# Two factor sets through memory, a finish by banks, and another order of the first phase

## The chip, the cores and the metric

The kernel runs on one core of a Trainium2 chip, in one launch. The time is the device time in microseconds (us) of that core. Five engines work in parallel, each through its own instructions in order, and wait for one another by semaphores: TensorE (PE; its weight loads are shown as PEld), VectorE (DVE), ScalarE (ACT), GpSimd (POOL), and SyncE (SP), which here only issues DMAs. A queue of DMAs belongs to the engine that issues them, and a waiting DMA holds up those behind it in the same queue.

## What is computed

Attention with a block mask, for 8 batches x 8 heads, 576 tokens and a head size of 64, then a two-layer network over all 4608 tokens:

```python
scores = scale * np.matmul(q, k.transpose(0, 1, 3, 2))        # scale = 1 / sqrt(64)
scores = np.where(block_i >= block_j, scores, -1000000000.0)  # blocks of 64 tokens
scores = scores - np.max(scores, axis=-1, keepdims=True)
attn = np.exp(scores)
attn = attn / (np.sum(attn, axis=-1, keepdims=True) + 1e-09)
out = np.matmul(attn, v)
# heads side by side: x is [4608, 512]
h = x @ w_in                                                  # w_in [512, 2048]
g = np.maximum(h, 0.0) + alpha * np.minimum(h, 0.0)
return g @ w_out                                              # w_out [2048, 512]
```

The reference makes the weights in 64 bits; they come as pairs of 32-bit words, and the kernel turns them into 32-bit numbers itself.

## The kernel before, in words

**Numbers.** Matrix products run on a rounded 32-bit format. A number that must not lose precision is split into a high part (a rounding copy, ACT, line 422) and a low part (number minus high part, POOL or DVE, line 423), and a product becomes three: high by high, high by low, low by high. A weight tile of 128 x 512 is first converted by `to_f32` (line 380): a DMA into a `raw` tile, then masks and bit operations on DVE (L398, L403, L406), conversions on ACT (L401, L409), a last multiplication on POOL (L417). One step in between, adding the lower word, has two forms, chosen by the conversion's priority (line 410): below `LOW_POOL` ACT converts the word (L411) and POOL adds it (L412); from there on one DVE instruction does both (L414). `RB`, `EB` and `EF` are the numbers of `raw`, `m` (result) and `ef` (intermediate) tiles.

**First phase.** 32 pairs of heads go through attention, one after another: scores on PE (L815), row maximum on DVE (L820), exchange of half rows on POOL (L792), exponential with row sum on ACT (L828), block transposes on DVE (L832), product with v on PE (L874). Four half pairs are done ahead of the loop, with priorities from `E0` and `E1`. `PM`, `PX`, `PT`, `PZ` and `PU` are priorities of the single steps against their pair, `VL` that of the load of v. Beside attention, 6 of the 16 blocks of 128 hidden units (`FA = 6`) are computed directly for chunks of 256 tokens (L518, L528, L530, L541, L544, L557), and their part of the result goes to memory (`part`, L750). Their twelve weight tiles are converted at the start (`first_weights`, line 428). The weights of the other ten blocks are converted meanwhile, tile k behind the pair `int(A0 + A1 * k)` (`weights_ahead`, line 444), and written to memory (`wd`). The priority of such a conversion is 5p + 100 where attention for pair p has 5p: it fills gaps.

**Second phase.** The remaining ten hidden blocks are taken as five pairs i = 0 to 4, and both layers use a scheme of seven products in place of eight (quadrants, and sums of quadrants). Each pair needs two factor sets, w1 and w2: two loads from `wd` (L454), four sums of 256 columns on POOL (`add`, L439), and four splits (512, 512, 512 and 256 columns) with the high parts on ACT and the low parts on DVE; a set is 2 x 7 x 256 numbers per partition. `later_weights` (line 457) makes all ten, for i = 0 to 4, w1 and w2 in turn. For each of nine chunks of 512 tokens, `factors` loads x from memory (L574), forms four differences (DVE, L583) and splits seven X factors. `pair1` (line 601) does seven products of six matmuls (L615), adds them up out of PSUM with the help of small `u` tiles (L624, L628, L635) and applies the activation (L528, L530). `parts_of` (line 657) makes from that the parts `ha` and `hs`: four sums of 128 columns (L439) and two splits. `pair2` (line 676) does the second layer's seven products, gathered over the five pairs in four PSUM banks M0/M1, M2/M3, M4/M5, M6 (L684); first the three that use `ha` (M0, M1, M6), then the four that use `hs` (M2 to M5). `finish` (line 693) then takes one copy (L706), seven sums (DVE, L703) and four sums with `part` (L439), and two stores to `out` (L718). In the last half chunk ("tail") the parts use spare X buffers, and the engines of their steps come from `TSADD`, `TALO` and `TSLO` in place of `SADD`, `ALO` and `SLO`.

**Memory.** When the last attention pair is done (`end_attention`, line 933), its memory becomes the pool `wb`: 4 w1 sets, 2 w2 sets, 4 X factors, 11 tiles `t2` (`WB1`, `WB2`, `XB2`, `TB2`). The direct blocks still have three chunks to go then. When these are done (`end_first`, line 947), their memory becomes `fx`: the remaining w1, w2, X and `t2`, `ha`, `hs`, and all 11 `u` tiles. An instruction that writes into new memory waits until the old users have finished, stores included.

**What sets the order.** Every instruction is entered in a plan with engine, cost, what it reads and writes, and a priority (smaller is earlier). `Plan.schedule` (line 140) plays the program through with those costs and takes for each free engine the ready entry of least priority for which buffers are free; the order in which it does so becomes each engine's order of instructions. On the chip an engine keeps this order also where the costs were off. Buffers of the kinds in `IN_ORDER` (line 78), the `mw` tiles of the loads from `wd` among them, are given out in the order in which the entries were made. `due(d)` (line 564) is a priority against the running count of PE's products in the second phase; `UX`, `UX0`, `UF`, `UP`, `UM`, `UO` and `UW` are such offsets, for X factors (`UX0`: those of the first chunk), `pair1`, parts, the sums of `finish`, its last sums, and weights.

## Time and profile before

| | us |
|---|---|
| median of 3 runs (1056.52 to 1058.59) | 1056.69 |
| the profiled execution | 1056.06 |
| its span, first to last instruction | 1054.3 |
| PE busy | 982.9 |
| DVE busy | 867.0 |
| POOL busy | 772.1 |
| ACT busy | 624.6 |

The profile comes from one execution. All times of the trace count from the span's first instruction. L422 is line 422 of the kernel before. Groups are named output<-input by the kernel's buffers, without their numbers: `w` stands for a factor set (w1 or w2), `t` for a `t2` tile, `bank` for a PSUM bank, `duo` for a pair of banks of attention. Matmuls are pipelined and their ends are modelled. What released a waiting instruction is inferred from semaphores; where several were waited for, the last by the profile is named.

### The profile page before, as it was taken

The numbers are of one execution on the slowest core, as the hardware profiler recorded it, in microseconds if no ns is written. First come the engines' busy times: TensorE is split into PE (matmuls) and PEld (weight loads), VectorE is DVE, ScalarE is ACT, GpSimd is POOL, SyncE is SP. The second block draws the span as 40 slices with busy tenths as digits, with TensorE's granted clock in tenths as the row PEclk, the third lists the DMA queues.
The fourth block names the chain that finished last, engine by engine and source line by source line (L and its number), as shares of the span: only waits on it lengthen the run. The fifth ranks groups of instructions, "written<-read, shape, count | busy, mean of one in ns | idle before, by whom it ended". The sixth has DMA issues, their size and how long they took to land. (4 is left out here: it accounts for less than half of the span.)

```text
span 1054.3 us, 34971 instructions
## 1 busy us (share of the span) xinstructions
PE 982.9 (93%) x13670; PEld 902.9 (86%) x13670; DVE 867.0 (82%) x1925; ACT 624.6 (59%) x2158; POOL 772.1 (73%) x1318
## 2 busy tenths in 40 slices
PE   5478999999999999999989799999999999999997
PEld 3366787889888898888878789999999999999996
DVE  6999889988888878866584997888888888888876
ACT  6878687877777676756554654445353545444442
POOL 5887567656566665646598889888887979797963
PEclk7679899999999999999999999999999999999999
DMA  8555667576566566442433202130303031221111
GB/s 311 157 194 172 220 215 239 168 245 204 181 217 224 184 194 204 154 164 77 131 103 110 72 21 81 42 100 22 101 21 100 25 98 44 78 61 62 61 42 60
DMA packets 85045, 135.96 MB, mean 129 GB/s; under 512 B 12176, under 2 KB 49552, under 8 KB 84880
## 3 DMA queue, kind: packets, MB, share of 16 engines
q1 hardware_dynamic: 84592, 133.59, 39.4%
q8 instruction: 107, 1.75, 0.7%
q14 instruction: 58, 0.48, 0.1%
q10 hardware_dynamic: 288, 0.14, 0.0%
HBM read 100.15 MB, written 33.55 MB: 127 GB/s over the span
## 5 line engine op out<-in xcount | busy, mean ns | idle before, releaser
L828 ACT ACTIVATE p<-duo,c 128x256 f32<-128x256 f32 (+8 forms) x576 | 221.1, 415 | 40.7 <-DVE c L823 32.2
L615 PE MATMUL bank<-X,w 128*128 128x256 f32 x1890 | 237.8, 282 | 3.1 <-DMA t<-wd 1.8
L615 PEld LDWEIGHTS bank<-X,w 128*128 128x128 f32 x1890 | 230.5, 190 | 4.3 <-ACT X L422 2.0
L792 POOL TENSOR_SCALAR c<-c 32x4 f32<-32x4 f32 (+3 forms) x400 | 100.6, 252 | 87.0 <-DVE c L820 59.4
L439 POOL TENSOR_TENSOR t<-t 128x128 f32<-128x128 f32 (+1 forms) x180 | 103.3, 583 | 60.5 <-DVE t L530 48.0
L684 PE MATMUL bank<-w,hs 128*128 128x256 f32 x1020 | 138.3, 284 | 5.5 <-POOL hs L423 5.5
L557 PE MATMUL bank<-wa,gh 128*128 128x512 f32 x432 | 137.9, 400 | 3.8 <-POOL gh L539 1.7
L684 PEld LDWEIGHTS bank<-w,hs 128*128 128x128 f32 x1020 | 128.9, 192 | 8.0 <-POOL hs L423 7.7
L828 ACT ACTIVATION_READ_ACCUMULATOR p<-duo,c 128x1 f32 x576 | 130.7, 228 | 0.0
L518 PE MATMUL bank<-xh,wa 128*128 128x256 f32 x864 | 126.7, 289 | 1.5 <-DVE g L530 1.3
L820 DVE TENSOR_REDUCE c<-duo 128x2 f32<-128x512 f32 (+8 forms) x288 | 121.3, 475 | 6.5 <-PE duo L815 6.2
L439 POOL TENSOR_TENSOR t<-t,t 128x128 f32<-128x128 f32 (+1 forms) x200 | 120.8, 609 | 4.0 <-DVE w L423 1.3
L518 PEld LDWEIGHTS bank<-xh,wa 128*128 128x128 f32 x864 | 114.5, 193 | 10.6 <-issue 3.4
L423 POOL TENSOR_TENSOR hs<-t,hs 128x512 fp32r<-128x512 f32 x85 | 112.1, 1319 | 13.2 <-ACT hs L422 13.0
L544 POOL TENSOR_TENSOR gl<-g,gh 128x256 fp32r<-128x256 f32 x108 | 85.1, 790 | 45.6 <-ACT gh L541 14.6
L422 ACT CAST hs<-t 128x512 fp32r<-128x512 f32 x85 | 52.8, 621 | 104.4 <-POOL t L439 103.4
L684 PE MATMUL bank<-w,ha 128*128 128x256 f32 x765 | 104.9, 283 | 5.8 <-DVE ha L423 5.8
L832 DVE STREAM_TRANSPOSE PTH<-p 128x576 f32<-128x576 f32 (+4 forms) x160 | 99.7, 630 | 11.6 <-ACT p L828 10.4
L815 PE MATMUL duo<-k,q 64*32 64x288 f32 (+4 forms) x2560 | 85.7, 382 | 22.6 <-ACT p L828 18.5
L684 PEld LDWEIGHTS bank<-w,ha 128*128 128x128 f32 x765 | 97.4, 191 | 6.2 <-DVE ha L423 6.2
L528 ACT ACTIVATE u<-bank 128x256 f32<-128x256 f32 x180 | 64.1, 382 | 62.6 <-DVE bank L628 62.3
L557 PEld LDWEIGHTS bank<-wa,gh 128*128 128x128 f32 x432 | 77.2, 188 | 22.7 <-issue 3.3
(69 smaller groups left out, 1913.2 us busy)
## 6 DMA issues: line engine op xcount, KB each, us to landing
v<-in_v SPq DMA_DIRECT2D x32, 576.0 KB, 4.2
k<-in_k SPq DMA_DIRECT2D x32, 288.0 KB, 5.3
t<-xd SPq DMA_DIRECT2D x36, 256.0 KB, 4.1
t<-part SPq DMA_DIRECT2D x36, 256.0 KB, 2.7
out<-t SPq DMA_DIRECT2D x36, 256.0 KB, 2.1
va<-in_v SPq DMA_DIRECT2D x32, 256.0 KB, 3.3
raw<-in_w_in SPq DMA_DIRECT2D x16, 512.0 KB, 5.3
raw<-in_w_out SPq DMA_DIRECT2D x16, 512.0 KB, 4.3
```

The source lines that it names most:

```text
L423: op(on, c_pool(n) + 60 if on == "POOL" else Beside(c_dve(n)), lambda: (nc.gpsimd if on == "POOL" else nc.vector).tensor_tensor(out=lo(), ...
L439: op(e, c_pool(n) if e == "POOL" else Beside(c_dve(n)), lambda: (nc.gpsimd if e == "POOL" else nc.vector).tensor_tensor(out=to[1](), in0=a ...
L518: nc.tensor.matmul(hp()[:, :n], ww()[:, 0, cc * P:(cc + 1) * P], x()[:, cc, :n], start=(i == 0 and cc == 0), stop=(i == 2 and cc == NCC - 1))
L544: op("POOL", c_pool(CHA) + 60, lambda: nc.gpsimd.tensor_tensor(out=gl(), in0=g(), in1=gh().bitcast(F32), op=ALU.subtract), r=[g, gh], w=[g ...
L557: nc.tensor.matmul(acc(), a()[:, ts], ww(), start=(first and i == 0), stop=(last and i == 2))
L615: nc.tensor.matmul(bank()[:, :CHA], W()[:, i, 256 * at + P * c:256 * at + P * c + P], B()[:, j, CHA * c:CHA * c + CHA], start=(n == 0), st ...
L684: nc.tensor.matmul(accs[n // 2]()[:, CHA * (n % 2):CHA * (n % 2) + CHA], b()[:, u, P * x:P * x + P], W()[:, v, 256 * W2AT[w]:256 * W2AT[w] ...
L792: nc.gpsimd.tensor_scalar(out=o, in0=i, scalar1=scale, scalar2=None, op0=ALU.mult)
L815: nc.tensor.matmul(sb()[32 * i:32 * i + 32, h, off[T]:off[T] + w], q()[hs, qs], blocks(k()[hs], T + 1, 32 * (i % 2)), start=True, stop=True)
L820: op("DVE", c_dve(2 * w), lambda t=t, w=w, o=o: nc.vector.tensor_reduce(out=c()[:, 0, 2 * t:2 * t + 2], in_=sb()[:, :, o:o + w], axis=AX.X ...
L828: op("ACT", 237 + w / 1.2, lambda x=2 * t + h, T=T, h=h, w=w, o=o: nc.scalar.activation(out=pb()[:, 2 * o + h * w:2 * o + h * w + w], in_= ...
L832: op("DVE", 85 + 2.08 * w, lambda to=to, a=a, w=w, o=o: nc.vector.transpose(out=to()[:, a:a + 2 * w], in_=pb()[:, 2 * o:2 * o + 2 * w]), r ...
```

## The change

**Stored factor sets.** `AGAIN` names two sets, w2 of pair 4 and w2 of pair 3. `later_weights`, now called after `end_first` has been entered, makes these two first, then the other eight in the old order. Each of the two is written to memory (`wf`) in two DMAs when it is complete, its buffer becomes free, and two DMAs fetch it into another w2 buffer once the old phase's memory is free (the key "fa"). The pool `wb` has 3 w1 sets, 2 w2 sets, 6 X factors, 12 `t2` and 2 `u` tiles; `fx` has the rest, the totals staying as they were. `XB` and `UX0` move the first chunk's X factors, `XWHEN` the loads of x for later chunks by one pair, `UX` and `UF` shift two priorities.

**Finish bank by bank.** In the last half chunk's last pair, `pair2` enters four groups of products, one for each bank, in place of two. In the last half chunk `finish` gives two of the four sums with `part` to POOL, and stores each half row by a DMA of its own, in turn on SP's and ACT's queue. The tail's steps get other engines (`TSADD`, `TALO`, `TSLO`).

**First phase.** `LOW_POOL` -100: every conversion takes the form with L414. Other priorities (`VL`, `E0`, `E1`, `PM`, `PZ`), another distribution of the later conversions (`A0`, `A1`), fewer tiles (`RB`, `EB`).

```diff
-LOW_POOL = 6
+LOW_POOL = -100
-VL = 0
-E0, E1 = -3, 2
+VL = 1.0
+E0, E1 = -2, 1.5
-A0, A1 = 2, 1.3
+A0, A1 = 3, 0.8
-XB = 5
+XB = 10
-XWHEN, UW, UX0 = 1, -30, -10
-UX, UF, UP, UM, UO = -8, 0, -5, -5, 20
-TSADD, TALO, TSLO = ("DVE", "DVE", "DVE", "DVE"), ("POOL",), ("DVE",)
-WB1, WB2, XB2, TB2, T2, UB = 4, 2, 4, 11, 14, 11
+XWHEN, UW, UX0 = 2, -30, -30
+AGAIN, UA, UL = ((1, 4), (1, 3)), -20, -20
+UX, UF, UP, UM, UO = -7, -4, -5, -5, 20
+TSADD, TALO, TSLO = ("POOL", "POOL", "POOL", "POOL"), ("DVE", "POOL"), ("DVE", "POOL")
+WB1, WB2, XB2, TB2, T2, UB, UB2 = 3, 2, 6, 12, 14, 11, 2
-RB, EB, EF = 4, 4, 6
+RB, EB, EF = 2, 3, 6
-PM, PX, PT, PZ, PU = -7, -4, -1, 0, -2
+PM, PX, PT, PZ, PU = -8, -4, -1, -1, -2
...
     def later_weights(prio):
-        for f in range(FA, NF, 2):
-            for i in range(2):
-                pr = prio((f - FA) // 2, i)
+        pairs = [(i, n) for n in range((NF - FA) // 2) for i in range(2)]
+        for i, n in [*AGAIN, *(x for x in pairs if x not in AGAIN)]:
+            for f in (FA + 2 * n,):
+                again = AGAIN.index((i, (f - FA) // 2)) if (i, (f - FA) // 2) in AGAIN else None
+                pr = prio((f - FA) // 2, i) + (UA if again is not None else 0)
...
+                if again is not None:
+                    (w1s, w2s)[i][f] = to = Buf(("w1", "w2")[i])
+                    for x in range(2):
+                        op("SP", 896, lambda W=W, x=x, again=again: nc.sync.dma_start(out=wf[again, x], in_=W()[:, x].bitcast(F32)), r=[((W, at), "hl"[x]) for at in (0, 2, 4, 6)], w=[("wf", again, x)], prio=pr)
+                    for x in range(2):
+                        op("SP", 896, lambda to=to, x=x, again=again: nc.sync.dma_start(out=to()[:, x].bitcast(F32), in_=wf[again, x]),
+                           r=[("wf", again, x), "fa"], w=[((to, at), "hl"[x]) for at in (0, 2, 4, 6)], claim=[to], prio=prio((f - FA) // 2, i) + UL)
...
-    def pair2(i, parts, accs):
+    def pair2(i, parts, accs, end):
...
-        for b, todo in ((ha, ((0, ha, 0, "11"), (1, ha, 2, "21"), (6, ha, 1, "t4"))),
-                        (hs, ((2, hs, 1, "t2"), (3, hs, 2, "t3"), (4, hs, 0, "t1"), (5, hs, 3, "22")))):
+        last3 = ((0, ha, 0, "11"), (1, ha, 2, "21")), ((2, hs, 1, "t2"), (3, hs, 2, "t3")), ((4, hs, 0, "t1"), (5, hs, 3, "22")), ((6, ha, 1, "t4"),)
+        for todo in last3 if end else ((*last3[0], *last3[3]), (*last3[1], *last3[2])):
+            b = todo[0][1]
...
-        for c, i, j in ((c11, 0, 0), (c22, 1, 1), (c12, 0, 1), (c21, 1, 0)):
-            add(OADD, CHA, ...
+        for k, (c, i, j) in enumerate(((c11, 0, 0), (c22, 1, 1), (c12, 0, 1), (c21, 1, 0))):
+            add(("POOL", "POOL", "DVE", "DVE")[k] if end else OADD, CHA, ...
+            if end:
+                queue, issuer = (("SP", nc.sync), ("ACTQ", nc.scalar))[k % 2]
+                op(queue, 128, lambda b=o[i], t=t0 + P - P * i, j=j, issuer=issuer: issuer.dma_start(out=out[t:t + P, CHA * j:CHA * j + CHA], in_=b()[:, CHA * j:CHA * j + CHA]),
+                   r=[(o[i], j)], prio=0)
-        for b, t in zip(o, (t0 + P, t0)):
+        for b, t in () if end else zip(o, (t0 + P, t0)):
...
-        rooms("wb", ..., ("t2", TB2, [512], F32))
+        rooms("wb", ..., ("t2", TB2, [512], F32), ("u", UB2, [CHA], F32))
...
-    later_weights(lambda n, i: ...)
...
-              ("ha", 2, [2, 3 * P], F32R), ("hs", 2, [2, 512], F32R), ("u", UB, [CHA], F32))
+              ("ha", 2, [2, 3 * P], F32R), ("hs", 2, [2, 512], F32R), ("u", UB - UB2, [CHA], F32))
...
-       ends=("wa", "xh", "xl", "xc", "xo", "g", "gh", "gl", "o"), prio=0, then=second_room)
+       ends=("wa", "xh", "xl", "xc", "xo", "g", "gh", "gl", "o"), w=["fa"], prio=0, then=second_room)
+    later_weights(lambda n, i: ...)
...
-                    pair2(i, parts_of(Rs[t0, i][h], i, h and t0 + CHB == TOK), accs)
-            finish(accs, t0 + CHA * h)
+                    pair2(i, parts_of(Rs[t0, i][h], i, h and t0 + CHB == TOK), accs, h and t0 + CHB == TOK and i == NG - 1)
+            finish(accs, t0 + CHA * h, h and t0 + CHB == TOK)
```

More of the change, by code (lines that the diff above doesn't have):

```diff
@@ L336, in attn_ffn @@
     part = dram.tile([TOK, DO], F32, name="part")
+    wf = dram.tile([max(len(AGAIN), 1), 2, P, 7 * 256], F32, name="wf")
     wd = dram.tile([2 * (NF - FA), P, 512], F32, name="wd")
@@ L691, in pair2, with finish @@
                r=[(b, "h"), (b, "l"), *[((W, W2AT[w] // 2 * 2), x) for *_, w in todo for x in "hl"]], w=[accs[n] for n in sorted({n // 2 for n, *_ in todo})], prio=1.0e6 + fseq[0])
-    def finish(accs, t0):
+    def finish(accs, t0, end):
         o = [Buf("t2", "ob") for _ in range(2)]
```

6 lines of the change are left out of this document (3 added, 3 removed).

## The prediction

> **What bounds the kernel now.** I read the page first: the span, the busy shares and the forty slices.
>
> ```profile
> span 1054.3 us, 34971 instructions
> PE 982.9 (93%) x13670; PEld 902.9 (86%) x13670; DVE 867.0 (82%) x1925; ACT 624.6 (59%) x2158; POOL 772.1 (73%) x1318
> PE   5478999999999999999989799999999999999997
> ```
>
> TensorE (PE) is the bound nearly everywhere: 1054.3 - 982.9 leaves 71.4 us of idle PE, and the slices put it at the start, at slices 20 to 22 and at the end. The busy table by stage gives each its size (columns: PE, weight load, DVE, ACT, POOL, granted clock, DMA share, GB/s).
>
> ```profile
> 0.00:106.00 106.00, 67.11 (x1702) 51.74 (x1707) 91.65 (x221) 82.27 (x338) 77.59 (x157) 0.75 0.63 209
> 7.00:70.00 63.00, 31.95 (x898) 23.73 (x888) 57.81 (x140) 52.90 (x224) 50.18 (x100) 0.66 0.64 217
> 70.00:106.00 36.00, 30.95 (x725) 24.74 (x713) 32.99 (x78) 27.88 (x113) 27.21 (x53) 0.88 0.62 196
> 106.00:330.00 224.00, 218.46 (x4561) 188.45 (x4547) 196.47 (x480) 170.96 (x729) 143.87 (x331) 0.99 0.66 211
> 520.00:575.50 55.50, 52.51 (x328) 45.98 (x327) 38.07 (x47) 29.48 (x68) 51.33 (x57) 1.00 0.40 125
> 575.50:606.00 30.50, 23.28 (x172) 22.22 (x171) 25.33 (x49) 16.71 (x39) 24.11 (x27) 0.94 0.33 98
> 650.00:1030.00 380.00, 376.25 (x3140) 374.66 (x3139) 319.26 (x680) 173.15 (x402) 320.84 (x429) 1.00 0.19 59
> 1030.00:1055.00 25.00, 16.63 (x135) 16.05 (x134) 16.52 (x43) 4.88 (x10) 7.50 (x6) 0.91 0.18 64
> ```
>
> So 38.9 us of the idle PE lies in the first 106 us, 3.0 + 7.2 = 10.2 us around the change of phase, 8.4 us in the tail, and 3.8 us in the 380 us of steady second phase, where only a new stall could change anything. The change touches all three places. Who PE waited for in the first 106 us, from the table of waits:
>
> ```profile
> PE duo L815 <- ACT p L828: 17.8, 5, 6.9
> PE duo L874 <- ACT p L828: 9.8, 3, 4.9
> ```
>
> The head is thus the softmax chain (DVE maximum, POOL swap, ACT exponential), with DVE the fullest of its engines: 57.81 of 63 us.
>
> **Head: conversions.** `LOW_POOL` -100 sends the six earliest weight conversions down the path that the others already take: six L411 (ACT) and six L412 (POOL) vanish, six more L414 appear on DVE. `RB` and `EB` cut what can be in flight (four raw tiles to two, four result tiles to three); `E0`, `E1`, `PM`, `PZ` only reorder. Rows by line (min/median/max, first and last start), then the DVE group of 7 to 70 us:
>
> ```profile
> L412 POOL TENSOR_TENSOR m<-m,ef x6: 1263/1272/1705, 16.7 to 55.1; 128x512 f32<-128x512 f32 x6
> L411 ACT ACTIVATE m<-raw x6: 643/660/684, 15.9 to 53.4; 128x512 f32<-128x512 uint32 x6
> L414 DVE SCALAR_TENSOR_TENSOR m<-raw,ef x26: 641/684/1769, 63.3 to 466.0; 128x512 f32<-128x512 uint32 x26
> L398 DVE TENSOR_SCALAR m<-raw 128x512 int32<-128x512 int32 x9 | 6.5, 717 | 0.0
> ```
>
> ACT loses 6 x 0.66 = 4.0 us, POOL 6 x 1.27 = 7.6 us, DVE gains 6 x 0.68 = 4.1 us, all before about 70 us. The price lies between -4.0 (ACT, for which PE waits, passes all its relief on) and +4.1 (DVE, which has 5.2 us idle there, passes all on); fewer buffers stay inside that, since conversions there wait for engines. I take +0.6, a little to the side of the fuller engine.
>
> The row for L398 shows more: a mean of 717 ns where an undisturbed one takes 376 (its shortest). The GPSIMD Engine Reference of the Trainium skill (section Specifications) says that GpSimd shares its SBUF interfaces with VectorE and that they contend when a DVE instruction has two SBUF inputs or runs in a 2-port mode. By that rule six fewer POOL instructions would also give DVE time back; with at most 9 x 0.34 = 3.1 us in that group to recover, an estimate of 1 us back, the sum would be 1.0 lower. The trace does not say which POOL instruction stretched which, and an L414 has two SBUF inputs itself, so I leave it out.
>
> **First phase: later conversions.** The twenty others move from pairs int(2+1.3k), the last at 26, to int(3+0.8k), the last at 18: by pair 18 all twenty have been offered instead of fourteen. Each costs DVE L398, L403, L406 and L414:
>
> ```profile
> L398 DVE TENSOR_SCALAR m<-raw x32: 376/420/1489, 10.3 to 455.5; 128x512 int32<-128x512 int32 x32
> L403 DVE TENSOR_SCALAR ef<-raw x32: 378/414/1523, 12.7 to 456.2; 128x512 int32<-128x512 int32 x32
> L406 DVE SCALAR_TENSOR_TENSOR ef<-raw,ef x32: 626/679/1794, 14.7 to 464.2; 128x512 int32<-128x512 int32 x32
> ```
>
> 0.42 + 0.41 + 0.68 + 0.68 = 2.2 us, so six of them 13.2 us. They carry a priority of 5p + 100 against 5p for attention, that is, they fill gaps. Their cover is DVE's idle time from 106 to 330 us, 224 - 196.5 = 27.5 us. I take 0. If that cover is gone, one instruction stands ahead of a softmax step per conversion, 6 x 0.68 = 4.1 us.
>
> **Change of phase.** PE, ACT, SP and DVE here, from the timeline (start, length, what; in brackets idle time and releaser):
>
> ```profile
> 575.46 3.03 PE L615 MATMUL bank<-X,w 128*128 128x256 f32 x24
> 580.30 1.71 PE L615 MATMUL bank<-X,w 128*128 128x256 f32 x10 [1.82 <-DMA t<-wd]
> 594.56 0.40 PE L684 MATMUL bank<-w,ha 128*128 128x256 f32 x2
> 599.89 1.71 PE L684 MATMUL bank<-w,ha 128*128 128x256 f32 x7 [4.93 <-DVE ha L423]
> 618.15 1.24 PE L684 MATMUL bank<-w,ha 128*128 128x256 f32 x9
> 576.39 1.09 SPq L750 DMA_DIRECT2D part<-o  x2
> 579.63 1.66 ACT L422 CAST X<-t 128x512 fp32r<-128x512 f32 x3 [3.27 <-DMA part<-o]
> 593.13 5.70 DVE L423 TENSOR_TENSOR w<-t,w 128x512 fp32r<-128x512 f32 x6
> 599.09 0.74 DVE L423 TENSOR_TENSOR ha<-t,ha 128x384 fp32r<-128x384 f32 x1
> 600.89 1.05 DVE L423 TENSOR_TENSOR w<-t,w 128x256 fp32r<-128x256 f32 x1
> ```
>
> PE issues four products (24 matmuls) and stops, because the last store of the first phase (SP, 576.39) must land before buffers in the old phase's memory can be written: three X factors and all u. With six X and two u in the memory that attention leaves, six products can go (36 matmuls, about 4.4 us, to 579.9), and only one X has to follow. I take the 1.82 us and the 0.18 + 0.28 us of X waits after it as gone but for 0.3: -2.0, bounds 0 and -2.3.
>
> The factor sets themselves do not get fewer: ten before and after, with four POOL sums, four ACT casts and four DVE subtractions each. What limits them before 575 us is POOL (51.33 of 55.5 us), so about as many are ready then: seven, from the 23 DVE subtractions of the first row below plus those that follow directly.
>
> ```profile
> L423 DVE TENSOR_TENSOR w<-t,w 128x512 fp32r<-128x512 f32 (+1 forms) x23 | 23.3, 1026 | 17.3 <-ACT w L422 17.1
> L423 DVE TENSOR_TENSOR w<-t,w 128x512 fp32r<-128x512 f32 (+1 forms) x16 | 13.6, 881 | 1.3 <-ACT w L422 1.1
> ```
>
> The first row is 520 to 575.5, the second 575.5 to 606. But two of the seven are now w2 sets that are not needed until pairs 3 and 4, stored and fetched again; a w1 set takes their place after 575. So the 13.6 us of subtractions, six of which stand ahead of `ha` and cost PE 4.93 us, remain: 0, bounds -4.93 (they move out of its way) and +3.4 (below). The new DMAs: four stores and four loads of 0.92 MB on SP. A store waits for a whole set, and behind it in SP's queue stand the loads of the next sets and the `part` stores; the loads, 3.67 MB at the 209 GB/s of the head's row, are 17.6 us, from 576.4 to 594, ahead of pair 3 (the row at 618.15). Cost 0 with that cover.
>
> **Tail.** The last pair's products go bank by bank, two sums move to POOL, four half stores go out on two queues.
>
> ```profile
> 1034.74 12.74 PE L684 MATMUL bank<-w,X 128*128 128x256 f32 x105
> 1041.80 1.36 DVE L423 TENSOR_TENSOR X<-t,X 128x512 fp32r<-128x512 f32 x1
> 1046.87 2.67 DVE L703 TENSOR_TENSOR u<-bank,u 128x256 f32<-128x256 f32 x7 [3.38 <-PE bank L684]
> 1049.45 1.42 DVE L439 TENSOR_TENSOR t<-t,u 128x256 f32<-128x256 f32 x4
> 1050.57 0.81 SPq L718 DMA_DIRECT2D out<-t  x2
> ```
>
> Now eleven DVE instructions, 1046.87 to 1050.87, follow the last matmul: 4.0 us. A matmul is 12.74 / 105 = 0.12 us, so bank 1 (M2, M3) ends nine matmuls, 1.1 us, ahead of the end; three of the seven sums are done by then plus 0.2. Left are four at 0.38 and DVE's own two at 0.36, 2.2 us: -1.8. The last store no longer queues behind another (0.81 / 2), less the POOL sum beside it: -0.2. Sum -2.0. The other side: all twenty small sums of the last half chunk go from DVE to POOL; DVE finished its last operand at 1043.16, and PE reaches that pair 21 matmuls before its end, at 1044.9, 1.8 us later. If POOL is later than that, up to +1.0.
>
> **Sum.** 0.6 + 0 - 2.0 + 0 - 2.0 = -3.4 against this execution's 1056.06 us (its span and 1.76 around it) gives 1052.7; it ran 0.6 under the median of 1056.69, so 1053.3.
>
> **Rivals.** (A) The last six subtractions no longer stand ahead of `ha`: 4.93 more, 1048.4. For it, two of the late sets come by DMA; against it, three are still built late. (B) Slower: DVE becomes the bound of the first phase. It is 92% busy from 70 to 106 us and 88% to 330; if it passes on the six L414 (4.1 instead of 0.6) and each earlier conversion delays a softmax step (4.1), and fewer raw buffers hold the weights of the first chunk one median conversion longer (2.2), the sum is -3.4 + 9.8 = +6.4, 1063. It decides from 97% of DVE in that stage. (C) The fourth w1 set is late. The second set after 575 now ends at 600.89 + 1.05; PE would want it 2 us before 594.56: a stall of 8.3 to 9.4 us where 4.93 stands, 3.4 to 4.4 more, so -3.4 + 3.4 = 0: 1056.7. (D) The tail gives nothing, since POOL's sums are late: 1055.3.
>
> **How the numbers follow.** Forecast 0.38, A 0.17, B 0.18, C 0.17, D 0.10. No change is what lies within 0.2%, 2.1 us, about what a measurement of this kernel can tell. A and most of the forecast (0.31; its own range is 1051 to 1055.5) are faster, 0.48; the rest of it, D and most of C (0.11) are the same, 0.28; B and the rest of C slower, 0.24. The range 1047 to 1062 takes in A and the body of B.
>
> **What would show it.** In the changed profile: no L411 or L412, 32 L414, and DVE from 7 to 70 us at 60 us or more; PE idle in the first 106 us still 37 to 42 us; six products in one piece at the change of phase; a wait of 4 to 6 us for `ha` or for a w1 set near 595; some 5.4 us instead of 7.4 (1046.87 to 1054.3) from the last matmul to the end. Wrong if the head moves by over 4 us, or if stages counted here at 0 (106 to 520, 606 to 1030) move by over 2.

## The result and the profile after

The changed kernel took 1066.68 us (median of 7 runs, 1064.72 to 1069.99), the kernel before on the same chip 1058.17 (1055.26 to 1062.08): a ratio of 1.0092, with a 95% interval of 1.0078 to 1.0107. It is slower, where the prediction said 1053.3 and most probably faster. The profiled execution took 1065.83 us with a span of 1063.4.

The new code moves the helper's lines: L831 and L890 are attention's products (L815, L874), L844 its exponential (L828), L626 and L695 the products of the second phase (L615, L684), L424 and L425 the high and low parts (L422, L423), L416 the form on DVE that was L414. The page's line of busy times:

```profile
PE 983.8 (93%) x13670; PEld 902.0 (85%) x13670; DVE 858.6 (81%) x1910; ACT 625.8 (59%) x2152; POOL 774.9 (73%) x1333
```

PE does as much work as before (983.8 against 982.9 us); it is idle 8.2 us longer. Two marks divide the 9.1 us of span into three: the first product of the second phase, and the first matmul of the tail's last pair. In PE's timeline (start, length, what, idle time and releaser):

```profile
581.80 4.47 PE L626 MATMUL bank<-X,w 128*128 128x256 f32 x36
587.57 0.74 PE L626 MATMUL bank<-X,w 128*128 128x256 f32 x4 [1.30 <-ACT X L424]
590.93 14.32 PE L626 MATMUL bank<-X,w 128*128 128x256 f32 x101 [2.62 <-POOL X L425]
...
1043.05 10.98 PE L695 MATMUL bank<-w,X 128*128 128x256 f32 x90
1054.62 0.51 PE L695 MATMUL bank<-w,X 128*128 128x256 f32 x2 [0.59 <-ACT X L424]
1055.35 1.82 PE L695 MATMUL bank<-w,X 128*128 128x256 f32 x13 [0.22 <-DVE X L425]
```

| | before | after | difference |
|---|---|---|---|
| start to first product of the second phase | 575.46 | 581.80 | +6.3 |
| from there to the tail's last pair | 459.28 | 461.25 | +2.0 |
| from there to the end | 19.56 | 20.35 | +0.8 |

The busy table by stage (columns as before) shows where the first phase loses:

```profile
7.00:70.00 63.00, 36.42 (x1018) 28.30 (x1011) 57.27 (x145) 49.45 (x219) 43.16 (x98) 0.76 0.66 218
70.00:106.00 36.00, 23.39 (x550) 18.95 (x534) 30.32 (x72) 25.84 (x104) 23.16 (x43) 0.81 0.50 160
106.00:330.00 224.00, 212.94 (x4477) 181.86 (x4476) 204.35 (x491) 172.92 (x729) 146.48 (x330) 0.99 0.71 226
```

From 7 to 70 us PE does 4.5 us more than before: the head gains. From 70 to 106 us it does 7.6 us less (23.39 against 30.95) and to 330 us another 5.5 less. The table of waits of the first 575 us names three things that are new or have grown: waits for `wa`, pauses put down to "issue" (PE waits for nothing that the profile shows), and one wait of 6.3 us, at 26 us, for a copy on ACT (`r`, L865). First after, only the larger rows of the first two:

```profile
PE duo L831 <- issue: 5.6, 5, 1.8
PE bank L529 <- ACT wa L424: 3.3, 1, 3.3
PE duo L890 <- issue: 2.9, 1, 2.9
PE bank L568 <- ACT wa L424: 2.2, 1, 2.2
PE bank L529 <- POOL wa L425: 1.2, 2, 0.9
...
```

The same table of before:

```profile
PE duo L815 <- issue: 1.8, 4, 0.6
...
PE bank L557 <- POOL wa L423: 0.9, 1, 0.9
...
```

Waits for `wa`, the split weights of the direct blocks, rise from 1.3 to 7.5 us in all; pauses without a releaser rise from 2.7 to 9.8 us. The wait for `r` has no row before; in turn the waits for `p`, the exponential, fall from 28.3 to 17.3 us. In all, PE's idle time up to the first product rises by 8.3 us (50.3 to 58.6). Of the second phase, the largest wait of after from 650 to 1036 us:

```profile
PE bank L626 <- ACT u L646: 7.3, 7, 1.1
```

The only one of before in the same stretch:

```profile
PE bank L684 <- POOL hs L423: 4.6, 8, 0.8
```

### The profile page after: what moved, and what is told of

It reads as the page before. It is cut to its first block, busy times and chain, and to the rows that moved or that the text cites. A ratio compares the mean times of both kernels' runs of the same rounds, so it can differ in the third digit from the quotient of the medians.

```text
span 1063.4 us, 35049 instructions
## 1 busy us (share of the span) xinstructions
PE 983.8 (93%) x13670; PEld 902.0 (85%) x13670; DVE 858.6 (81%) x1910; ACT 625.8 (59%) x2152; POOL 774.9 (73%) x1333
## 3 DMA queue, kind: packets, MB, share of 16 engines
q8 instruction: 107, 1.75, 0.7%
## 4 chain that ended last, share of the span: by engine, by line
PE 55%; POOL 21%; DVE 8%; issue 7%; ACT 6%; DMA 2%; SPq 0%; POOLq 0%; ACTq 0%; DVEq 0%
PE bank L626 14%; PE bank L695 13%; PE bank L529 9%; PE bank L568 8%; POOL t L441 7%; PE duo L831 6%; PE duo L890 5%; POOL X L425 3%; ACT p L844 3%; POOL hs L425 3%; POOL c L808 2%; POOL gl L555 2%; DVE c L836 2%; POOL z L808 1%; POOL xl L517 1%
## 5 line engine op out<-in xcount | busy, mean ns | idle before, releaser
L844 ACT ACTIVATE p<-duo,c 128x256 f32<-128x256 f32 (+8 forms) x576 | 221.6, 412 | 70.6 <-DVE c L839 63.5
L626 PE MATMUL bank<-X,w 128*128 128x256 f32 x1890 | 239.7, 284 | 11.5 <-ACT u L646 7.3
L626 PEld LDWEIGHTS bank<-X,w 128*128 128x128 f32 x1890 | 231.8, 191 | 14.4 <-ACT u L646 8.7
L441 POOL TENSOR_TENSOR t<-t 128x128 f32<-128x128 f32 (+1 forms) x190 | 105.9, 566 | 61.1 <-DVE t L541 53.9
L695 PE MATMUL bank<-w,hs 128*128 128x256 f32 x1020 | 138.1, 283 | 2.5 <-POOL hs L425 1.9
L695 PEld LDWEIGHTS bank<-w,hs 128*128 128x128 f32 x1020 | 127.7, 190 | 5.7 <-POOL hs L425 5.7
L441 POOL TENSOR_TENSOR t<-t,t 128x128 f32<-128x128 f32 (+1 forms) x210 | 128.4, 619 | 4.7 <-DVE w L425 2.1
L844 ACT ACTIVATION_READ_ACCUMULATOR p<-duo,c 128x1 f32 x576 | 128.6, 224 | 0.0
L425 POOL TENSOR_TENSOR hs<-t,hs 128x512 fp32r<-128x512 f32 x85 | 112.7, 1326 | 13.8 <-ACT hs L424 13.8
L695 PE MATMUL bank<-w,ha 128*128 128x256 f32 x765 | 103.6, 282 | 0.0
L424 ACT CAST hs<-t 128x512 fp32r<-128x512 f32 x85 | 52.8, 621 | 84.0 <-POOL t L441 74.4
L695 PEld LDWEIGHTS bank<-w,ha 128*128 128x128 f32 x765 | 96.6, 190 | 0.0
L831 PE MATMUL duo<-k,q 64*32 64x288 f32 (+4 forms) x2560 | 81.3, 368 | 13.0 <-ACT p L844 7.4
```

The costliest lines, as they stand in the source:

```text
L425: op(on, c_pool(n) + 60 if on == "POOL" else Beside(c_dve(n)), lambda: (nc.gpsimd if on == "POOL" else nc.vector).tensor_tensor(out=lo(), ...
L441: op(e, c_pool(n) if e == "POOL" else Beside(c_dve(n)), lambda: (nc.gpsimd if e == "POOL" else nc.vector).tensor_tensor(out=to[1](), in0=a ...
L626: nc.tensor.matmul(bank()[:, :CHA], W()[:, i, 256 * at + P * c:256 * at + P * c + P], B()[:, j, CHA * c:CHA * c + CHA], start=(n == 0), st ...
L695: nc.tensor.matmul(accs[n // 2]()[:, CHA * (n % 2):CHA * (n % 2) + CHA], b()[:, u, P * x:P * x + P], W()[:, v, 256 * W2AT[w]:256 * W2AT[w] ...
L831: nc.tensor.matmul(sb()[32 * i:32 * i + 32, h, off[T]:off[T] + w], q()[hs, qs], blocks(k()[hs], T + 1, 32 * (i % 2)), start=True, stop=True)
L844: op("ACT", 237 + w / 1.2, lambda x=2 * t + h, T=T, h=h, w=w, o=o: nc.scalar.activation(out=pb()[:, 2 * o + h * w:2 * o + h * w + w], in_= ...
```

## The experiments

All ratios are against the kernel before, run on the same chip, with 95% intervals. "First product" and "tail" are the first and the last line of the table above, "middle" the one between, each from one profiled execution.

| run | median us | ratio | first product | middle | tail |
|---|---|---|---|---|---|
| first_only | 1063.68 | 1.0058 [1.0041, 1.0076] | 581.66 | 459.4 | 19.6 |
| rest | 1058.24 | 1.0010 [0.9998, 1.0022] | 574.67 | 459.8 | 20.0 |
| finish_only | 1056.29 | 0.9997 [0.9982, 1.0012] | 578.74 | 458.0 | 20.1 |
| stored_oldprio | 1053.30 | 0.9968 [0.9948, 0.9987] | 575.04 | 456.3 | 19.5 |
| f_low | 1067.63 | 1.0090 [1.0066, 1.0113] | 585.13 | 461.1 | 19.5 |
| f_a | 1060.10 | 1.0028 [1.0016, 1.0040] | 574.27 | 462.0 | 19.5 |
| f_rb | 1059.44 | 1.0032 [1.0017, 1.0047] | 580.12 | 459.6 | 19.6 |
| f_order | 1061.97 | 1.0048 [1.0031, 1.0066] | 580.84 | 459.7 | 19.6 |
| b_lessv | 1056.22 | 1.0001 [0.9989, 1.0014] | 574.70 | 459.4 | 19.5 |
| f_low_lessv | 1065.40 | 1.0084 [1.0068, 1.0101] | 584.04 | 459.8 | 19.6 |
| best | 1051.28 | 0.9958 [0.9942, 0.9973] | 573.36 | 456.0 | 18.7 |
| stored_uf | 1052.27 | 0.9959 [0.9943, 0.9975] | 574.54 | 456.1 | 19.5 |
| b_dve2 | 1060.87 | 1.0032 [1.0018, 1.0046] | 579.74 | 460.0 | 19.5 |
| b_more | 1062.71 | 1.0052 [1.0039, 1.0064] | 580.41 | 459.3 | 19.6 |
| stored_xwhen | 1064.62 | 1.0073 [1.0043, 1.0103] | 575.57 | 467.7 | 19.5 |
| stored_ux | 1053.30 | 0.9966 [0.9953, 0.9978] | 575.41 | 456.0 | 19.6 |
| first_rb4 | 1061.66 | 1.0048 [1.0031, 1.0065] | 581.50 | 458.3 | 19.5 |
| after_mended | 1059.49 | 1.0024 [1.0009, 1.0040] | 583.03 | 456.9 | 18.6 |

The first product of one execution can be off by 2 or 3 us: that of `finish_only`, whose first phase is the old one, came at 578.74 with a ratio of 1. The eight kernels with the old first phase (`rest`, `finish_only`, the four `stored_` ones, `best` and the one before) have PE idle for 49.1 to 52.7 us up to there, and busy, with the same matmuls, for 522.4 to 528.9. So parts of the first phase are judged by ratios, and profiles are used for what a wait is, not for the last microsecond.

### Which of the three changes costs

`first_only` is the kernel before with the settings of the first phase; `rest` is the changed kernel without them; the two others take one further part each.

```diff
 # first_only, against the kernel before
+LOW_POOL = -100
+VL = 1.0
+E0, E1 = -2, 1.5
+A0, A1 = 3, 0.8
+RB, EB, EF = 2, 3, 6
+PM, PX, PT, PZ, PU = -8, -4, -1, -1, -2
 # rest: these lines as before, all else as changed
 # finish_only, against the kernel before: the code of finish and pair2, and
+TSADD, TALO, TSLO = ("POOL", "POOL", "POOL", "POOL"), ("DVE", "POOL"), ("DVE", "POOL")
 # stored_oldprio: AGAIN, XB, UX0, WB1 to UB2 and the code of the stored sets, with
+XWHEN, UW, UX0 = 1, -30, -30
+UX, UF, UP, UM, UO = -8, 0, -5, -5, 20
```

> The kernel before with the first phase's settings alone (LOW_POOL -100, VL, E0, E1, A0, A1, RB 2, EB 3, PM, PZ); factor sets, priorities of the second phase and finish as before. Theory F (these settings cost the first phase its time: in the changed kernel the second phase's first product starts at 581.8 us against 575.5): 6 us slower than the kernel before, ratio 1.005 to 1.008, first product of the second phase near 582. Rival S (the stores and extra set work around 520 to 575 us cost it): within 1 us of the kernel before, first product near 575.5.

> The changed kernel with the first phase's settings put back: stored sets, second phase's priorities, tail's engines and finish as changed. Theory F: the second phase's part of the loss alone, which the two traces put at +2.0 (start of its first product to start of the last half chunk's) and +0.8 (from there to the end), so 0 to 3 us over the kernel before, ratio 1.000 to 1.003. Rival S: 6 to 9 us over, ratio 1.006 to 1.009.

> The kernel before with the finish by banks and the tail's engines alone. The prediction on record: -2.0 us, PE not waiting in the last half chunk. The reading of the changed kernel's trace: PE waits 0.8 us for the last pair's hs, whose sums POOL ends at 1053.9, and that eats most of a gain near 1 us: -1 to 0 us, PE idle some 0.8 us in the last half chunk.

> The kernel before with the stored factor sets and the memory that goes with them alone (AGAIN, WB1, XB2, TB2, UB2, XB, UX0); XWHEN, UX and UF, finish and first phase as before. Theory P (the new wait of PE for the copy to u, 7.3 us in seven of the chunks after 650 us, comes from UF -4, UX -7 and XWHEN 2): that wait is gone, and the change of phase's gain stays, -3 to -4 us. Rival M (it comes from the stored sets' memory, fewer u tiles at the right place): the wait is there, 0 us or slower.

The first phase alone costs 0.4 to 0.8%, 4.3 to 8.0 us. The rest with it undone is no faster than before, the finish is worth nothing as it stands, and the stored sets gain 1.4 to 5.5 us once `XWHEN` and the two priorities are as before. So there are three findings to explain: the first phase, the settings of the second phase, the tail.

### The second phase: which setting makes PE wait for `u`

```diff
 # all three: the stored sets on the old first phase and the old finish
 # stored_uf
+XWHEN, UW, UX0 = 1, -30, -30
+UX, UF, UP, UM, UO = -8, -4, -5, -5, 20
 # stored_xwhen
+XWHEN, UW, UX0 = 2, -30, -30
+UX, UF, UP, UM, UO = -8, 0, -5, -5, 20
 # stored_ux
+XWHEN, UW, UX0 = 1, -30, -30
+UX, UF, UP, UM, UO = -7, 0, -5, -5, 20
```

> The kernel before with the stored sets, and UF -4 in place of 0 (XWHEN and UX as before). Theory U (UF makes PE wait for the copy to u in the steady second phase, some 7 us): slower by 3 to 4 us than with UF 0, so about the time of the kernel before, with that wait in seven chunks. Rival X (it is XWHEN or UX): no such wait, 3 us faster than the kernel before.

> Stored factor sets on the old first phase and the old finish, with UX -8 and UF 0 as before, and XWHEN 2 alone from the new settings. If XWHEN makes the seven waits of some 7 us in all of a first product for the copy of u on ACT: they stand in the profile, and the time is 1055 to 1058. If UX makes them: no such wait, 1052 to 1054.

> The same with XWHEN 1 and UF 0 as before, and UX -7 alone from the new settings. If UX makes the seven waits for the copy of u: they stand in the profile, 1055 to 1058. If XWHEN makes them: 1052 to 1054. If neither alone does: both kernels lie at 1052 to 1054, and only the two together cost it.

`stored_uf` and `stored_ux` are as fast as `stored_oldprio`. `stored_xwhen` is slower than before, more than expected, and its waits from 650 to 1030 us are the ones in question:

```profile
PE bank L626 <- ACT u L646: 6.9, 7, 1.1
PE bank L695 <- DVE ha L425: 3.3, 1, 3.3
```

`XWHEN` 2 is the cause. What it does shows in the changed kernel's timeline around one of the seven waits, on ACT, POOL and PE:

```profile
731.99 0.62 ACT L424 CAST hs<-t 128x512 fp32r<-128x512 f32 x1 [1.30 <-POOL t L441]
732.52 0.37 ACT L718 COPY u<-bank 128x256 f32<-128x256 f32 x1
732.78 0.51 ACT L424 CAST ha<-t 128x384 fp32r<-128x384 f32 x1
733.19 0.37 ACT L646 COPY u<-bank 128x256 f32<-128x256 f32 x1
...
727.75 1.74 POOL L425 TENSOR_TENSOR X<-t,X 128x512 fp32r<-128x512 f32 x1
...
731.19 1.19 POOL L441 TENSOR_TENSOR t<-t,t 128x128 f32<-128x128 f32 x2
...
733.62 0.98 PE L626 MATMUL bank<-X,w 128*128 128x256 f32 x6 [1.08 <-ACT u L646]
```

x is loaded one pair later, and the plan gives ACT another order. POOL splits an X factor (727.75) ahead of the sums from which `hs` is made; ACT waits 1.30 us for these sums; the copy of `u` is three places behind that cast in ACT's order; PE needs a bank that this copy frees. In `stored_oldprio` POOL splits an X factor ahead of the sums too (724.07), but ACT makes the copy ahead of the cast (724.09 and 726.13), and PE runs on through six products (36 matmuls from 723.18) without a wait. One setting of a load thus reaches PE over POOL and ACT, once a chunk. The 4.6 us of short waits for `hs` that it replaces were there before. In `stored_xwhen` the middle is 11.4 us longer than in `stored_oldprio`; the two rows, 10.2 us, stand for 5.6 of that. PE's busy time from the first product to the tail is 6.2 us longer as well (450.1 against 443.9), of which some 1.7, an estimate (0.17 x 10), go with a granted clock of 0.83 from 800 to 810 us, right behind the wait for `ha` (1.00 from 650 to 790 us); the rest is not explained. Its nine executions lie far apart, 1058.81 to 1071.72 us. In `rest` and in the changed kernel, which have the two priorities as well, the middle is 3.5 and 5.0 us longer (459.8 and 461.25 against 456.3).

### The tail, and a kernel that beats both

```diff
 # best, against the kernel before: the stored sets as in stored_oldprio with
 # XWHEN, UX and UF as before, and the finish by banks, but in the tail
+TSADD, TALO, TSLO = ("DVE", "DVE", "DVE", "DVE"), ("POOL",), ("DVE",)
```

> The kernel before with the stored sets (memory as changed, XWHEN, UX and UF as before) and the finish by banks with the tail's engines as before. If the 0.8 us wait in the tail comes from POOL's sums (TSADD, TALO, TSLO), it is gone, and the finish's gain near 1 us adds to the 3.4 us of the stored sets: 4 to 5 us faster than the kernel before. Rival: the finish gives nothing by itself: 3.4 us, as without it.

`best` takes 1051.28 us, 0.3 to 0.6% less than before: the lowest median of the study, though its ratio can't be told from that of `stored_uf`. Its last products and sums:

```profile
1029.33 12.73 PE L695 MATMUL bank<-w,X 128*128 128x256 f32 x105
...
1041.09 2.67 DVE L715 TENSOR_TENSOR u<-bank,u 128x256 f32<-128x256 f32 x7 [3.01 <-PE bank L695]
...
```

PE has no gap here. In the changed kernel (first fence) it has two, because the tail's small sums now run on POOL, one after another; the last of POOL, ACT and DVE before the gaps are:

```profile
1052.92 1.00 POOL L441 TENSOR_TENSOR t<-t,t 128x128 f32<-128x128 f32 x2
...
1053.95 0.62 ACT L424 CAST X<-t 128x512 fp32r<-128x512 f32 x1 [3.67 <-POOL t L441]
...
1054.60 0.69 DVE L425 TENSOR_TENSOR X<-t,X 128x512 fp32r<-128x512 f32 x1 [2.39 <-ACT X L424]
```

ACT waits 3.67 us for POOL, and DVE 2.39 us for the cast that ACT then makes. So the finish by banks is worth 0.9 us of tail (19.56 to 18.67) and the engines of the tail take 1.4 back (20.0 in `rest`).

### The first phase, part by part

```diff
 # f_low, against the kernel before
+LOW_POOL = -100
 # f_a
+A0, A1 = 3, 0.8
 # f_rb
+RB, EB, EF = 2, 3, 6
 # f_order
+VL = 1.0
+E0, E1 = -2, 1.5
+PM, PX, PT, PZ, PU = -8, -4, -1, -1, -2
```

> The kernel before with LOW_POOL -100 alone. Theory D (the prediction's slower rival: DVE takes six more instructions where it is fullest): 3 to 4 us slower, PE idle in the first 106 us up by that. Rival R (fewer tiles for conversions) and rival O (priorities): within 1 us of the kernel before.

> The kernel before with A0 3 and A1 0.8 alone (later conversions offered from pair 3 to 18 in place of 2 to 26). Theory D: up to 4 us slower, PE idle from 106 to 330 us up from 5.5 to about 10. Rivals R and O: within 1 us, PE idle there 5 to 7 us.

> The kernel before with RB 2 and EB 3 alone (two raw tiles, three result tiles). Theory R (the twelve first conversions go through too few tiles, so that products of the first chunks wait for their weights and hold up attention's products behind them on PE): 4 to 6 us slower, the last of the twelve low parts later than 110 us, PE waits for wa near 70 to 115 us. Theory D and rival O: within 1 us.

> The kernel before with the first phase's priorities alone (VL 1, E0 -2, E1 1.5, PM -8, PZ -1). Rival O (the order: the first pair done 10 us earlier, at 59 in place of 69 us, before the weights are there, and the steps of a pair in another order): 4 to 6 us slower. Theories D and R: within 1 us, either side.

Each part alone makes the kernel slower: by ratios 0.90, 0.28, 0.32 and 0.48%, 2.0% in all, where all together cost 0.58%. They don't add; the new settings were a set, and `LOW_POOL` alone costs more than all of them together. Which wait costs `f_a` its 0.28% its profile doesn't show: it comes from the fastest of its runs (1057.61 us), and PE's idle time from 106 to 330 us is 9.3 us, as theory D expected (before 5.5), but 50.9 us up to the first product, as before (50.3). `f_rb` shows what fewer raw and result tiles do; its table of waits of the first 575 us has

```profile
PE bank L529 <- ACT wa L424: 10.1, 3, 4.8
```

against 0.4 + 0.9 us for `wa` before. With two raw and three result tiles the weights of the direct blocks come late, and PE stands ahead of three groups of direct products, which begin at 68, 84 and 99 us.

### VectorE's work at the head, in the old order

```diff
 # b_dve2, against the kernel before (L398, and L403 in the same way)
-        op("DVE", Beside(350), lambda: nc.vector.tensor_scalar(
+        op("DVE", Beside(350), lambda: [nc.vector.tensor_scalar(
...
-            out=mb().bitcast(I32), in0=high(), scalar1=0x7FF00000, scalar2=None, op0=ALU.bitwise_and),
+            out=mb().bitcast(I32), in0=high(), scalar1=0x7FF00000, scalar2=None, op0=ALU.bitwise_and) for _ in range(2 if prio < 6 else 1)][-1],
```

> The kernel before with one thing more: in the six earliest weight conversions, L398 and L403 are issued twice (the same result twice). Every engine keeps its order; VectorE gets 6 x (0.42 + 0.41) = 5.0 us more of work by the medians of before, all ahead of about 60 us, a little more than the 4.1 us of the six L414 that LOW_POOL -100 puts there. Theory D (VectorE's work at the head is on the path, whatever the order): the time rises by 4 to 5 us, 1060 to 1062, about half of what LOW_POOL -100 costs alone. Theory O (the loss comes from the new order that the plan makes for everything behind, not from the work itself): within 2 us of before, and PE's idle time from 106 to 330 us stays at 5 to 7 us where it is 14.7 with LOW_POOL -100.

The time rises by 0.18 to 0.46%, 1.9 to 4.9 us, and theory D is right on the place: PE waits longer in the first 106 us, and little longer behind them (0.7 us to 330 us and 1.3 from there to the first product). Its rows in the busy table by stage:

```profile
0.00:106.00 106.00, 61.85 (x1637) 48.78 (x1637) 92.63 (x227) 79.59 (x329) 76.44 (x152) 0.75 0.64 206
106.00:330.00 224.00, 217.78 (x4503) 186.52 (x4503) 197.78 (x480) 172.26 (x734) 145.13 (x331) 0.99 0.67 211
```

And its three largest waits of the first 120 us, where the same rows of before have 17.8, 9.8 (the prediction's fence) and 2.9:

```profile
PE duo L831 <- ACT p L844: 18.9, 5, 7.0
PE duo L890 <- ACT p L844: 11.0, 3, 5.6
PE duo L831 <- DVE xc L896: 6.0, 3, 4.3
```

PE does 5.3 us less by 106 us (61.85 against 67.11), about the 5.0 us of added work, and DVE is still only 92.63 of 106 us busy. DVE's idle time there is little slack: of its 5.2 us from 7 to 70 us in the kernel before, its own table of waits puts 4.8 down to POOL, ACT and PE, the other engines of the chain of softmax. But `f_low` is not this: its idle PE time is 35.1 us up to 106 us, less than the 38.9 before, and 14.7 from 106 to 330 us against 5.5. So what `LOW_POOL` costs comes later, where the six conversions are long done; that it comes out of the order that the plan makes from it is the reading that is left, and no run shows it by itself.

### PE's pauses without a releaser

Of `f_low`'s 14.7 us from 106 to 330 us, some 7 are pauses; in the first 575 us it has 11.8 us of them, nearly all in these two rows:

```profile
PE duo L890 <- issue: 6.1, 3, 2.7
PE duo L831 <- issue: 4.9, 8, 2.0
```

The trace has a DMA queue that fits PE's instructions alone, 107 packets of 16384 bytes (1.75 MB, which is 64 bytes for each of 13670 matmuls and 13670 weight loads, of which one packet holds 256); in the page's table of queues, packets, MB and share:

```profile
q8 instruction: 107, 1.75, 0.7%
```

One pause of the changed kernel, of 1.84 us, ends at 173.79, and such a packet ran from 171.46 to 172.38. The traces show that this is no chance. If PE's records (matmuls, weight loads, its sequencer's waits) are counted in the order of their starts, 94 of the 98 pauses of 0.3 us or more ahead of the second phase, in all twenty traces, end at a record whose number leaves 193 or 194 when divided by 256, and 1.2 to 1.8 us after a packet landed: the first instructions of a new packet. A packet starts at most 297 records ahead of the record that needs it (211 to 246 in the median, by trace), so PE has about one packet in hand. The four others, of 2.3 to 3.4 us, stand elsewhere, among them the longest of the changed kernel. It is in PE's and DVE's timeline:

```profile
82.80 0.43 DVE L848 STREAM_TRANSPOSE PTL<-p 128x128 f32<-128x128 f32 x2
83.33 0.97 PE L890 MATMUL duo<-PTL,va 64*64 64x128 f32 x17 [2.85 <-issue]
```

Its first weight load starts 0.07 us after DVE's last transpose of PTL has ended (83.30 and 83.23): a wait for DVE that the table doesn't name. `first_only`, `f_low` and `f_low_lessv` have one such wait each. Without them the pauses are 7.0 us in the changed kernel and 9.5 in `f_low`.

Three runs tried whether the other transfers make these packets late. The two with less traffic bring in 64 KB of one load of v in place of 576 KB from the seventh pair on, and so leave out part of v. The third copies v once more, from memory to memory, for nobody.

```diff
 # b_lessv (against the kernel before) and f_low_lessv (against f_low)
-nc.sync.dma_start(out=v(), in_=vT[p])
+nc.sync.dma_start(out=v(), in_=vT[p]) if p < 6 else nc.sync.dma_start(out=v()[:, :1], in_=vT[p, :, :1])
 # b_more, against the kernel before
+(nc.sync.dma_start(out=v(), in_=vT[p]), nc.sync.dma_start(out=vd[p % 8], in_=vT[p]))
```

> The kernel before; from the seventh pair on, the load of v brings one of its nine blocks in place of all (64 KB in place of 576 KB; the other blocks keep an earlier pair's values, so this leaves that part of attention's input out). Orders of all engines' instructions unchanged. Theory I (PE's waits that the trace puts down to 'issue', 2.7 us in the first phase here and 11.8 us with LOW_POOL -100, are its instruction stream arriving late behind full DMA engines): issue waits under 1.5 us, time 1 to 3 us less. Theory D (DVE): the time as the kernel before.

> The kernel before with LOW_POOL -100 alone, and from the seventh pair on one of v's nine blocks loaded in place of all (the same input left out). Theory I: PE's issue waits behind the seventh pair nearly vanish (those from about 160 us on, some 5 us; those before it, some 6.6 us, stay), and the time is 4 to 6 us under that with the whole v; against the kernel before with the small v 4 to 6 us are left. Theory D: still 8 to 10 us over the kernel before.

> The kernel before with one more transfer of 576 KB per pair of heads on SP's queue, v from memory to memory, which nothing reads; every other engine keeps its order. It adds 32 x 0.59 = 19 MB, some 35 to 40 GB/s to the 211 GB/s of the first phase. Theory I (PE's pauses without a releaser, the instruction refills, come late when the data transfers take nearly all of the DMA engines): the sum of such pauses in the first phase, 2.7 us before, rises to 6 to 12 us, and the time by about as much, 1060 to 1067. Rival (the pauses have to do with the order of PE's instructions, not with the load of the DMA engines): the pauses stay at 2 to 5 us; the time stays within 2 us unless loads of q and k come late, which the waits would name.

Less traffic did not give the time back: `f_low_lessv` is still 0.84% slower than before. Its pauses from 160 us on, behind the seventh pair, fall from 5.2 to 2.4 us; in `b_lessv` they stay (2.5 and 2.4). More traffic alone did raise them, with every other engine's order as before: from 2.7 to 9.3 us, and the time by 0.39 to 0.64%; its waits for loads do not rise (`qa`: 1.7 us, before 2.9).

```profile
PE duo L832 <- issue: 5.3, 8, 2.2
PE duo L891 <- issue: 2.9, 2, 2.3
...
```

(L832 and L891 are attention's products.) Its longest pause, in PE's timeline:

```profile
137.62 2.46 PE L891 MATMUL duo<-PTH,v 64*64 64x160 f32 x45 [2.31 <-issue]
```

The DMA queues from 135.1 to 136.3 us (packets, MB, share of 16 engines):

```profile
q1 hardware_dynamic: 226, 0.46, 98.5%
q8 instruction: 1, 0.02, 5.0%
```

Between 129.1 and 135.1 us no packet of q8 runs; one starts at 135.23, while the data queue takes 98.5% of the engines, and PE, which paused in the middle of a group at 135.3, goes on 1.4 us after it has landed. So these pauses are late instruction refills, by their place in PE's order and in time, and a higher load of data transfers made more of them. The load alone doesn't decide: `f_a` has a mean share from 106 to 220 us of 0.74, nearly that of `b_more` (0.75), and 0.8 us of pauses, and kernels with the same old first phase had 1.2 to 5.2 us in their single profiles. That it matters where the bursts fall is likely, and not shown.

The Trainium skill (Runtime: NRT & Kernel Launch, Instruction fetch mechanics) says that an engine's instructions are refilled in blocks of 16 KiB, 256 instructions, by a DMA queue of the sequencer, and that crossing a block is mostly hidden. The packets of this trace agree in size; "mostly hidden" holds for most of the 107 and not for the ones above, up to 1.84 us each in the changed kernel.

### Undoing the tiles, and three settings at once

```diff
 # first_rb4, against first_only
-RB, EB, EF = 2, 3, 6
+RB, EB, EF = 4, 4, 6
 # after_mended, against the changed kernel: the same, and
+XWHEN, UW, UX0 = 1, -30, -30
+TSADD, TALO, TSLO = ("DVE", "DVE", "DVE", "DVE"), ("POOL",), ("DVE",)
```

> The kernel before with the new settings of the first phase, but RB 4 and EB 4 as before (four raw tiles, four result tiles). With RB 2 and EB 3 as well, PE waits 7.4 us from 70 to 120 us for weights of the direct blocks (wa); before 1.3. Theory W (the smaller number of raw and result tiles makes these weights late, and that is most of what the first phase loses): the waits for wa in that stretch fall to 1 to 3.5 us, the first product of the second phase comes at 576 to 578 in place of 581.7, and the time lies at 1056 to 1059. Rival (the six L414 and the refills carry the loss, and PE would only wait for something else): 1062 to 1064, as with all the new settings of the first phase, with the time spent on softmax and on pauses without a releaser.

> The changed kernel with three settings undone: RB 4 and EB 4, XWHEN 1, and the old engines of the tail's steps. If the losses found singly add up (the waits for u by XWHEN 2, the waits for wa by the fewer tiles, POOL's late sums in the tail): no wait of a first product for the copy of u, no wait for X in the tail, and 1052 to 1056, still above the kernel that leaves the whole first phase as before (1051.3). If the first phase keeps its loss in another form: 1058 to 1061.

Theory W falls. With the old numbers of tiles the waits for `wa` drop from 7.4 to 4.3 us and the pauses happen to drop from 10.2 to 3.1, and yet the first product comes at 581.50 and the time is 1061.66, a ratio that can't be told from that of `first_only` (a gain of some 3.6 us, an estimate from the two intervals, is not excluded). Part of the answer is other waits in the first 575 us, where `first_only` has 7.8 us on the first line and none on the second:

```profile
PE duo L831 <- ACT p L844: 13.9, 8, 5.3
PE bank L529 <- DVE g L541: 3.8, 5, 1.5
```

The other part is no wait: up to the first product PE is idle for 55.3 us where it was 59.7 in `first_only`, and busy for 526.2 where it was 522.0, with the same matmuls. That busy time differs by more between kernels with one and the same first phase (522.4 to 528.9, above), so the 4.2 us say nothing of the tiles, and single profiles can't show how much of the 4.4 us of idle time arrives.

`after_mended` removes the waits for `u` and those of the tail: middle and tail (456.9 and 18.6) are nearly those of `best`. Only the first phase is as late as ever (583.03), and the time, 1059.49, is above the kernel before by 0.1 to 0.4%.

**What stays open.** That the first phase's new settings cost some 4 to 8 us as a set is shown, that each part alone costs time, from 1.7 to 11.9 us, too, and so is that VectorE's work at the head, fewer tiles and more transfers each cost 2 to 7 us when put in alone. No single one of them carries the loss: with one taken away, the loss stood elsewhere. Which property of the new order makes that so was not found.

## Why the prediction was wrong, by its steps

**Conversions at the head: +0.6 taken, bounds -4.0 and +4.1.** This is the step that failed, together with the next. The value was set just above the middle, a little to the side of the fuller engine, as if DVE's 5.2 us of idle time would hide most of the work. `b_dve2` shows that this idle time hides little: of 5.0 us more work on DVE, 1.9 to 4.9 arrive in the time. So for work added with nothing relieved the upper bound was nearer the truth than the middle. But the six L414 come with relief for ACT and POOL, and at the head itself `f_low` gains: 3.8 us of idle PE by 106 us, near the lower bound. `LOW_POOL` alone nonetheless costs 7.0 to 11.9 us, above the upper bound, because the loss comes from 106 to 330 us (14.7 us of idle PE against 5.5), where the sum had 0: it priced the instructions that move, and not the order that follows for everything behind them. In the changed kernel, too, most of it lies there: idle PE rises by 2.7 us up to 106 us and by 5.6 from there to 330 us.

The rule of the Trainium skill that was weighed there (GPSIMD Engine Reference, Specifications: interfaces shared with VectorE) agrees in direction, and with more than the 1 us that I had estimated. The groups of 7 to 70 us in `f_low` (L400 is the old L398, L405 the old L403, L408 the old L406), where POOL has less to do:

```profile
L416 DVE SCALAR_TENSOR_TENSOR m<-raw,ef 128x512 f32<-128x512 uint32 x8 | 8.1, 1017 | 0.0
L408 DVE SCALAR_TENSOR_TENSOR ef<-raw,ef 128x512 int32<-128x512 int32 x8 | 5.6, 702 | 0.4 <-ACT ef L403 0.4
L405 DVE TENSOR_SCALAR ef<-raw 128x512 int32<-128x512 int32 x8 | 3.9, 493 | 0.0
L400 DVE TENSOR_SCALAR m<-raw 128x512 int32<-128x512 int32 x8 | 3.1, 393 | 0.0
```

and in the kernel before:

```profile
L406 DVE SCALAR_TENSOR_TENSOR ef<-raw,ef 128x512 int32<-128x512 int32 x8 | 7.9, 981 | 0.2 <-ACT ef L401 0.2
...
L403 DVE TENSOR_SCALAR ef<-raw 128x512 int32<-128x512 int32 x8 | 5.7, 710 | 0.0
...
L414 DVE SCALAR_TENSOR_TENSOR m<-raw,ef 128x512 f32<-128x512 uint32 x2 | 2.4, 1212 | 0.0
```

L400 takes 393 ns in the mean, where L398 took 717 (6.5 us, quoted in the prediction); L416 takes 1017. The four groups sum to 20.7 us with eight L416; before they were 22.5 with two L414 and one L398 more. So the six added instructions cost DVE nothing in the sum from 7 to 70 us, and the time rose all the same. Which instruction of POOL stretched which the trace does not say.

**Fewer tiles: "fewer buffers stay inside that, since conversions there wait for engines".** Wrong: with fewer raw and result tiles alone PE waits for weights (`f_rb`: 10.1 us for `wa`, 1.8 to 5.0 us of time).

**"`E0`, `E1`, `PM`, `PZ` only reorder".** No term stood for them; with `VL` they cost 3.3 to 7.0 us alone.

**Later conversions: 0, other bound +4.1.** Alone 1.7 to 4.2 us: the bound held and the value taken did not. The cover of 27.5 us of idle DVE was not enough of a cover; where the loss arises `f_a`'s profile doesn't show.

**Rival B** had the place (the first phase) and the sign. Its time, 1063 for the whole change, lies 3.7 us under the 1066.68, and that it comes so near is luck: it priced the first phase at 10.4 us, which alone measured 4.3 to 8.0, and the rest at -4.0, which measured none. Its mechanism was not as told: it was to decide from a DVE at 97% in 70 to 106 us, and DVE has 30.32 of 36 us there, 84%. DVE from 7 to 70 us at 60 us or more did not show either (57.27). Idle PE up to 106 us was to be 37 to 42, and is 41.6; the movement of the head by over 4 us that was to refute came later, between 106 us and the change of phase.

**Change of phase: -2.0, with the stall of `ha` left in place.** The six products in one piece came as said (36 matmuls, 4.47 us; 4.4 predicted). Rival A's part came as well: no wait for `ha`. In their place stand 2.62 and 1.30 us for X factors, which are late next. Idle time from the first product to 650 us goes from 9.7 to 6.1 us, -3.6: better than the forecast by 1.6 and 3.3 short of A. C did not come: nothing waits for a w1 set. PE's busy time gave part back, with a granted clock of 0.89 from 575.5 to 606 us against 0.94 before.

```profile
575.50:606.00 30.50, 25.71 (x172) 24.03 (x172) 25.73 (x49) 15.78 (x36) 23.97 (x30) 0.89 0.66 225
...
650.00:1030.00 380.00, 372.15 (x3078) 367.26 (x3077) 308.09 (x664) 172.71 (x394) 317.52 (x421) 1.00 0.19 61
```

**Steady second phase: counted at 0.** Idle PE there rises by 3.3 us from 650 us to the tail (4.6 to 7.85), beyond the 2 that were to refute. The step that failed is an omission: `XWHEN` moves a load, and the work that hangs on it was not followed through POOL and ACT, though the prediction quoted the row that says that only a new stall could change anything there.

**Tail: -2.0, other bound +1.0.** Rival D is what happened: POOL's sums are late, and the tail is 0.8 us longer. Without the engine change the finish by banks is worth 0.9 and not 2.0. The prediction took all eleven of DVE's sums, 4.0 us, to follow the last matmul; its own rows end that matmul at 1034.74 + 12.74 = 1047.48, 0.6 us after the sums begin. In `best` they begin not much earlier: they start only 1.0 us ahead of the end of PE's last matmul (1041.09 against 1042.06), so that two sums saved on DVE are most of the gain.

**The sum.** With the terms as measured in the changed kernel: +6.3 for the first phase, -3.6 and +3.3 for the waits around the change of phase and after it, 2.3 of busy time between the first product and the tail, +0.8 for the tail, 9.1 in all, where -3.4 stood. Most of it came from the first phase; but the rest, at +2.8 in these profiles and a ratio of 1.0010 in `rest`, did not gain the 4.0 us that it was to bring either.

## What to carry to other kernels

An engine that is 90% busy in a serial chain may have little slack in its last 10%: where the chain's steps alternate between engines, added work on one of them can count nearly in full, however idle it looks (1.9 to 4.9 of 5.0 us here). Settings that were tuned as a set could not be priced one by one here, neither before the run nor by runs; the ones of the steady stage deserve the same walk through each queue as the ones where the stall is, since a load moved by one step reached PE over POOL and ACT. And of a change with several parts, the part that pays can be taken alone: stored sets and the finish by banks with the old settings are 0.3 to 0.6% faster than before, most of it by the stored sets.

## What the runs showed of the hardware that I had not expected

PE can stop in the middle of a group of matmuls where a refill of its instructions comes late: refills of 16384 bytes, each for 256 instructions, about every 6.5 us in the first phase, each starting at most 297 records ahead of its need. A refill takes about 1 us under way, and the pause around a late one was up to 2.9 us (`f_low_lessv`); the sum in a first phase went from 0.8 to 9.5 us in the profiles here, and rose from 2.7 to 9.3 us when only an idle copy of 576 KB per pair was added. In the profile such a pause is idle time of PE with the releaser "issue", but not every such row is one: a refill shows by its place, at every 256th record.
